# Decode block: the second part of w_up loaded in eleven smaller loads instead of one

## The chip, the cores and the metric

The kernel runs on one core of a Trainium2 chip. The metric is the device time of one execution in microseconds; before the change it is 204.33 us, the median of three runs (204.2, 204.33 and 204.76).

## The reference

One token goes through one block of a transformer in decode mode, all in bf16 at the boundary:

- x is one row of D = 640 numbers. It is normalised (layernorm without weights) and multiplied by wq (640 x 4096), which gives 32 queries of 128 numbers, one per head.
- Every head has its own cache of 4096 keys and 4096 values of 128 numbers. scores = q k / sqrt(128), softmax over the 4096 positions, and the weighted sum of the values.
- The 32 results together (4096 numbers) are multiplied by wo (4096 x 640) and added to x: this is h.
- h is normalised, g = h w_gate and u = h w_up (both 640 x 1728), gelu(g) * u is multiplied by w_down (1728 x 640) and added to h. This is the output, 640 numbers.

```python
h = x + _A_ref(_layernorm(x, axis=-1), A_k_cache, A_v_cache, A_wq, A_wo)
h2 = h + _B_ref(_layernorm(h, axis=-1), B_w_gate, B_w_up, B_w_down)
```

Each byte of the caches and of the weights is used once. They are about 84 MB.

## The kernel before

**How the program is written.** A small class `Sched` (L45) keeps five lists, one for each engine and one for SyncE (SP). `S.op` adds an instruction to an engine's list, `S.dma` adds a load, and both take the list of tokens that it must wait for. A token is a semaphore's name and a value. Each load slot has its own semaphore, named after the slot ("wu0", "wu1"). A wait that the engine has already made is left out. At the end the five lists are written out in the order in which they were filled. All loads but that of x are issued by SP, so the order of `S.dma` calls in the text is the order in which SP issues them.

**Attention.** The 32 heads are worked in NG = 8 groups of four. In a group each partition has 128 of the positions of one head. The keys of a group come in one load of 4 MB into `kbuf` (two buffers), the values in one load of 4 MB into `vbuf` (two buffers). For a group, `mult` (DVE, L324) multiplies the keys by the query, `fold` and `red` add the products up, `soft` makes the weights and `values` (PE, L380) applies them. `kfree[g]` is the token of the last `mult` of group g, `vfree[g]` that of its last `values`: a later load into the same buffer waits for it.

**The weights of the second half** have no room of their own. `wg_sb` (w_gate) lies over one key buffer, `wu_sb` (w_up) over the other, `wd_sb` (w_down) over a value buffer, `wo_sb` over that of wq. So their loads wait until the last groups have left these buffers. `wu_sb` is 128 partitions x 5 x 1728: partition p holds the rows 5p to 5p+4 of w_up.

**The loads at the end,** in the order of SP's list: three quarters of wo (L549); the values of the last group in two parts (L256); the last quarter of wo (L549); w_gate in one load (`pieces`, L543); w_up in two loads, rows 0 to 2 of each partition and rows 3 and 4 (`pieces` with the cuts [0, 3, 5], L543); and w_down: its last 64 rows (L561), then parts of 8, 4 and 1 blocks of 128 rows (L566). The loads of w_up wait for `kfree[7]`, those of w_down for `vfree[6]`. In the second load of w_up a partition takes 2 x 1728 numbers that lie in one piece in memory, 6912 bytes, and there are 128 such rows.

**Who uses them.** `up` (L617) multiplies the five pieces of h by w_gate, and then by w_up: for each of the five c in turn 14 matmuls, whose first waits for the token d_w[c]. So the 43rd of 70 matmuls with w_up is the first that needs the second load. PE's order after it: the rest of `up`, a small matmul with `twice` for the last 64 rows, and `down` (L659), which waits for each part of w_down. DVE's `hm` (L643) needs the whole of `up`. A last copy (L663) and a store of four rows (L664) end the kernel.

Of the kernel before, what the change touches and what calls it, by code (L numbers as in the profile page):

```python
# [16 lines left out]
NC_D = D // 128  # L17
# [6 lines left out]
NG = H // HG  # L24
# [85 lines left out]
def bass_sequential_preLN__gqa_block_cached__glu_gated_geglu__decode_kernel(  # L110
# [12 lines left out]
    S = Sched(nc)  # L123
# [10 lines left out]
    def over(name, base, shape):  # L134
        return nc.alloc_sbuf_tensor_at(name, shape, BF16, offset=nc.lookup_mloc(base).addr)
# [4 lines left out]
    wu_sb = over("wu_sb", kbuf[(NG + 1) % 2], [128, NC_D, DF])  # L140
# [88 lines left out]
    a = S.op("vector", lambda v: v.reduce_sum(  # L229
        jred[:, :], I32[:, :].rearrange("p (j c) -> p j c", c=HW), axis=AX.X))  # L230
    b = S.op("vector", lambda v: v.reduce_sum(
        cred[:, :], I32[:, :].rearrange("p (j c) -> p c j", c=HW), axis=AX.X))
# [11 lines left out]
    kfree, vfree = [None] * NG, [None] * NG  # L244
# [26 lines left out]
    def layernorm(src, t_src, o, dst, ps, beside=None):  # L271
        b = S.op("vector", lambda v: v.scalar_tensor_tensor(  # L272
            out=sq[:, :], in0=src[:, :], scalar=1.0, in1=src[:, :], op0=ALU.mult, op1=ALU.mult,
            accum_out=st[:, o + 1:o + 2]), [t_src])
        c = S.op("tensor", lambda t: t.matmul(ps[:, 0:2], part[:, :], st[:, o:o + 2],  # L275
                                              start=True, stop=True), [b, t_part])
        if beside is not None:
            beside()
        q = 2 * o
        d = S.op("vector", lambda v: v.scalar_tensor_tensor(  # L280
            out=ln[:, q:q + 1], in0=ps[:, 0:1], scalar=ps[:, 0:1], in1=eps[:, :],
            op0=ALU.mult, op1=ALU.subtract, reverse1=True), [c])
        e = S.op("scalar", lambda a: a.activation(  # L283
            ln[:, q + 1:q + 2], ps[:, 1:2], ACTF.Ln, bias=ln[:, q:q + 1]), [d])
        f = S.op("scalar", lambda a: a.activation(
            ln[:, q + 2:q + 3], ln[:, q + 1:q + 2], ACTF.Exp, scale=-0.5), [e])
        return S.op("vector", lambda v: v.tensor_scalar(  # L287
            dst[0], dst[1], ps[:, 0:1], ln[:, q + 2:q + 3], ALU.subtract, ALU.mult), [f])
# [250 lines left out]
    def pieces(slot, dst, src, cuts, waits):  # L539
        toks = []  # L540
        for i in range(len(cuts) - 1):
            lo, hi = cuts[i], cuts[i + 1]
            tok = S.dma("sync", "%s%d" % (slot, i), lambda s, lo=lo, hi=hi: s.dma_start(  # L543
                dst[:, lo:hi, :], src[:, lo:hi, :]), waits)
            toks += [tok] * (hi - lo)
        return toks

    def load_wo(lo, hi):
# [8 lines left out]
    d_wg = pieces("wg", wg_sb, B_w_gate[:, :].rearrange("(p c) n -> p c n", c=NC_D),  # L557
                  [0, 5], [kfree[NG - 2]])
    d_wu = pieces("wu", wu_sb, B_w_up[:, :].rearrange("(p c) n -> p c n", c=NC_D),
                  [0, 3, 5], [kfree[NG - 1]])  # L560
    d_wdr = S.dma("sync", "wdr", lambda s: s.dma_start(  # L561
        wd_sb[:, NFT, 0:D // 2], B_w_down[NFT * 128:DF, :].rearrange("r (h n) -> (r h) n", h=2)), [vfree[NG - 2]])
    d_wd = []
# [11 lines left out]
    def project(w):  # L575
        tok = None
        for c in range(HW):
            for cc in range(NC_D):
                last = w == NW - 1 and c == HW - 1 and cc == NC_D - 1
                first = w == 0 and c == 0 and cc == 0  # L580
                tok = S.op("tensor", lambda t, c=c, cc=cc, first=first, last=last: t.matmul(  # L581
                    pp[:, cc:cc + 1], wo_sb[:, w, c, cc::NC_D], aP[:, w * HW + c:w * HW + c + 1],
                    start=first, stop=last, skip_group_check=True),
                    [t_aP[w], d_wo[w], red_done[NG * NP - 2]], token=last)
        return tok
# [10 lines left out]
    b = project(w)  # L596
# [17 lines left out]
    t_hln = layernorm(h32, t_h, 2, (hln[:, :], h32[:, :]), pz, residual)  # L614


    def up(ps, w, d_w):  # L617
        b = None
        for c in range(NC_D):
            for s in range(NF):  # L620
                first = c == 0 and s == 0
                last = c == NC_D - 1 and s == NF - 1
                part = w[:, c, DF - 128:DF]
                if s < NFT:
                    b0, n, k = WD_COLS[s]
                    part = w[:, c, b0 + k:b0 + 128 * n:n]
                b = S.op("tensor", lambda t, s=s, c=c, part=part, first=first, last=last: t.matmul(
                    ps[:, s:s + 1], part, hln[:, c:c + 1],
                    start=first, stop=last, skip_group_check=True), [t_hln, d_w[c]], token=last)
        return b  # L630

    t_g = up(pg, wg_sb, d_wg)
    t_u = up(pu, wu_sb, d_wu)
    a = S.op("vector", lambda v: v.tensor_copy(g_t[:, :], pg[:, 0:NF]), [t_g])
    a = S.op("vector", lambda v: v.tensor_mul(t1[:, :], g_t[:, :], g_t[:, :]), [a])
    a = S.op("vector", lambda v: v.tensor_mul(t2[:, :], t1[:, :], g_t[:, :]), [a])
    a = S.op("vector", lambda v: v.scalar_tensor_tensor(
        out=t3[:, :], in0=t2[:, :], scalar=GELU_C1, in1=g_t[:, :], op0=ALU.mult, op1=ALU.add), [a])
    a = S.op("scalar", lambda a: a.activation(e_t[:, :], t3[:, :], ACTF.Exp, scale=-2.0 * GELU_C0), [a])
    a = S.op("vector", lambda v: v.tensor_scalar(d_t[:, :], e_t[:, :], 1.0, 0.0, ALU.add, ALU.add), [a])  # L640
    a = S.op("vector", lambda v: v.reciprocal(r_t[:, :], d_t[:, :]), [a])
    a = S.op("vector", lambda v: v.tensor_mul(gu[:, :], g_t[:, :], r_t[:, :]), [a])
    t_hm = S.op("vector", lambda v: v.tensor_mul(hm[:, :], gu[:, :], pu[:, 0:NF]), [a, t_u])  # L643

    b = S.op("tensor", lambda t: t.matmul(
        pz[:, 32:33], twice[:, :, :], hm[:, NFT:NF], start=True, stop=True), [t_hm, t_tw])
# [3 lines left out]
    def down(s, j):  # L650
        if s == NFT:
            return hr[:, j // 2:j // 2 + 1], wd_sb[:, NFT, j % 2 * NQ:(j % 2 + 1) * NQ]
        return hm[:, s:s + 1], wd_sb[:, s, j * NQ:(j + 1) * NQ]

    order = list(range(WD_PARTS[0])) + [NFT] + list(range(WD_PARTS[0], NFT))
    for i, s in enumerate(order):
        for j in range(4):
            last = i == NF - 1
            b = S.op("tensor", lambda t, s=s, j=j, last=last: t.matmul(  # L659
                pd[32 * j:32 * j + 1, 0:NQ], *down(s, j),  # L660
                start=False, stop=last, skip_group_check=True),
                [t_hr if s == NFT else t_hm, d_wd[s]], token=(last and j == 3))
# [35 lines left out]
```

## Time and profile before

| what | value |
|---|---|
| median of three runs | 204.33 us (204.2 to 204.76) |
| the profiled execution | 204.18 us, its span 202.9 us |
| TensorE's granted clock, mean | 0.919 |
| busy: PE, DVE, ACT | 77%, 57%, 15% of the span |
| read from memory | 84.23 MB, 415 GB/s over the span |
| second load of w_up | 864 KB, 26.4 us from issue to landing |
| loads of w_down | 23.4, 24.5 and 24.4 us from issue to landing; the last 64 rows 20.7 us |

All times below are of the profiled execution, in microseconds from the start of its span, if nothing else is said. A line of the chain or of the timeline begins with its start and its length. "SPq" is the queue of SP that issues loads; a line of it tells how long the issue took, not the transfer. In a line of the timeline the part in brackets is the engine's idle time before it and what ended it. The trace also keeps each DMA packet with its start, length and size (one packet is one row of a load, or a landing mark of 4 bytes), and the times at which a load's landing marks arrive: sixteen to a load of 128 rows, one from each DMA engine.

### The profile page before, as it was taken

Reading aid. Unit: us, or ns where it says so; the run is one execution under the profiler, and the core shown is the slowest. Engines: PE = TensorE matmul, PEld = TensorE weight load, DVE = VectorE, ACT = ScalarE, POOL = GpSimd, SP = SyncE. Lnnn points to the kernel's source line nnn. Section 1 sums busy time; section 2 is a strip of 40 time slices with the busy share of each in tenths; the row PEclk is TensorE's granted clock in tenths of the full one; section 3 lists DMA queues with packets and bytes.
Section 4 is the critical chain, followed back from the end, with each engine's and each line's share of the span. In section 5 each row is a group of like instructions: output and inputs, shape, how many; then the busy total and the mean of one; then the engine's idle time right before and its main releaser. Section 6 shows DMA issues by size and latency. Waiting matters only on the chain.

```text
span 202.9 us, 2478 instructions
## 1 busy us (share of the span) xinstructions
PE 155.8 (77%) x1069; PEld 73.2 (36%) x1075; DVE 115.9 (57%) x150; ACT 30.6 (15%) x110; POOL 1.2 (1%) x7
## 2 busy tenths in 40 slices
PE   0003649689959967999999499979768999996784
PEld 0001113233324322443343134424323344796682
DVE  5002087998099629883992588469999422301130
ACT  2000210006003300240060005100604013000000
POOL 1000000000000000000000000000000000000000
PEclk9999999999999996999999879999999999955555
DMA  6999999999999999999999999999999899999992
GB/s 250 420 460 413 413 439 465 439 413 413 436 446 452 420 409 420 436 434 459 413 413 426 452 449 420 420 420 420 471 433 423 381 430 458 404 422 417 415 420 87
DMA packets 4306, 84.38 MB, mean 416 GB/s; under 512 B 584, under 2 KB 840, under 8 KB 1096
## 3 DMA queue, kind: packets, MB, share of 16 engines
q1 hardware_dynamic: 4152, 84.23, 97.2%
q8 instruction: 8, 0.13, 0.3%
q10 hardware_dynamic: 144, 0.00, 0.0%
q14 instruction: 2, 0.02, 0.0%
HBM read 84.23 MB, written 0.00 MB: 415 GB/s over the span
## 4 chain that ended last, share of the span: by engine, by line
DMA 54%; DVE 28%; PE 14%; ACT 1%; issue 1%; SPq 0%
DMA kbuf<-in_A_k_cache_dram 34%; DVE prod L324 19%; DMA wd_sb<-in_B_w_down_dram 12%; DMA x_sb<-in_A_x_dram 8%; DVE sc L340 4%; PE pf L333 4%; PE pg L380 4%; PE pu L380 3%; PE pq L303 2%; DVE xz L397 2%; DVE xm L394 1%; ACT qb L309 1%; DVE mx L348 1%; DVE xb L287 0%; PE pf L659 0%
## 5 line engine op out<-in xcount | busy, mean ns | idle before, releaser
L324 DVE TENSOR_TENSOR prod<-kbuf,qb 128x4096 bf16<-128x4096 bf16 x32 | 72.8, 2278 | 32.8 <-DMA kbuf<-in_A_k_cache_dram 26.1
L333 PE MATMUL pf<-prod,Ibf 128*128 128x512 bf16 x256 | 65.7, 404 | 20.2 <-DVE prod L324 20.2
L333 PEld LDWEIGHTS pf<-prod,Ibf 128*128 128x128 bf16 x256 | 24.1, 102 | 58.9 <-DVE prod L324 26.8
L380 PE MATMUL pg<-vbuf,P 128*16 128x512 bf16 x128 | 29.9, 379 | 0.0
L340 DVE TENSOR_REDUCE sc<-pf 128x32 f32<-128x512 f32 x32 | 21.6, 676 | 5.1 <-PE pf L333 5.1
L380 PE MATMUL pu<-vbuf,P 128*16 128x512 bf16 x96 | 22.6, 384 | 0.0
L365 ACT ACTIVATE nb<-pm 128x4 f32<-128x4 f32 x8 | 1.4, 174 | 115.6 <-PE pm L362 115.6
L369 ACT ACTIVATE P<-sc,nb 32x128 bf16<-32x128 f32 x32 | 18.5, 578 | 0.9
L380 PEld LDWEIGHTS pg<-vbuf,P 128*16 128x16 bf16 x128 | 10.6, 89 | 14.5 <-issue 1.3
L275 PE MATMUL pz<-st,part 128*128 128x2 f32 x4 | 1.2, 363 | 17.2 <-DVE sq L272 17.2
L303 PE MATMUL pq<-wq_sb,xb 128*128 128x512 bf16 x34 | 10.8, 452 | 3.8 <-DVE xb L287 1.8
L380 PEld LDWEIGHTS pu<-vbuf,P 128*16 128x16 bf16 x96 | 8.3, 91 | 12.1 <-issue 2.3
L309 ACT CAST qb<-pq 32x128 bf16<-32x128 f32 x32 | 8.2, 257 | 6.5 <-PE pq L303 5.8
L369 ACT ACTIVATION_READ_ACCUMULATOR P<-sc,nb 32x1 f32 x32 | 8.0, 251 | 0.0
L581 PE MATMUL pf<-aP,wo_sb 128*128 128x1 bf16 x160 | 7.0, 178 | 0.7 <-issue 0.4
L290 DVE SCALAR_TENSOR_TENSOR x<-x_sb 128x5 f32<-128x5 bf16 x1 | 0.2, 166 | 12.7 <-DMA x_sb<-in_A_x_dram 12.7
L397 DVE TENSOR_REDUCE xz<-xm 16x128 f32<-16x512 f32 x7 | 7.3, 1040 | 0.2
L581 PEld LDWEIGHTS pf<-aP,wo_sb 128*128 128x128 bf16 x160 | 6.9, 132 | 1.2 <-issue 0.9
L275 PEld LDWEIGHTS pz<-st,part 128*128 128x128 f32 x4 | 1.0, 312 | 17.3 <-DVE sq L272 17.3
L303 PEld LDWEIGHTS pq<-wq_sb,xb 128*128 128x128 bf16 x40 | 3.8, 111 | 7.9 <-ACT qb L309 2.1
L283 ACT ACTIVATE ln<-pz,ln 128x1 f32<-128x1 f32 x2 | 0.5, 262 | 34.8 <-DVE ln L280 34.8
L394 DVE TENSOR_TENSOR xm<-pg,rmask 16x512 f32<-16x512 f32 x4 | 2.7, 671 | 3.4 <-PE pg L380 3.4
(78 smaller groups left out, 66.0 us busy)
## 6 DMA issues: line engine op xcount, KB each, us to landing
kbuf<-in_A_k_cache_dram SPq DMA_DIRECT2D x8, 4096.0 KB, 25.1
vbuf<-in_A_v_cache_dram SPq DMA_DIRECT2D x7, 4096.0 KB, 23.0
wq_sb<-in_A_wq_dram SPq DMA_DIRECT2D x1, 5120.0 KB, 15.3
wo_sb<-in_A_wo_dram SPq DMA_DIRECT2D x1, 3840.0 KB, 28.7
vbuf<-in_A_v_cache_dram SPq DMA_DIRECT2D x1, 3072.0 KB, 12.7
wg_sb<-in_B_w_gate_dram SPq DMA_DIRECT2D x1, 2160.0 KB, 22.2
wu_sb<-in_B_w_up_dram SPq DMA_DIRECT2D x1, 1296.0 KB, 24.8
wo_sb<-in_A_wo_dram SPq DMA_DIRECT2D x1, 1280.0 KB, 17.5
```

The source lines that it names most:

```text
L275: c = S.op("tensor", lambda t: t.matmul(ps[:, 0:2], part[:, :], st[:, o:o + 2], start=True, stop=True), [b, t_part])
L303: tok = S.op("tensor", lambda t, c=c, n0=n0: t.matmul(pq[:, :], xb[:, c, :], wq_sb[:, c, n0:n0 + HG * DH], start=(c == 0), stop=(c == NC_D ...
L309: t_qb[g] = S.op("scalar", lambda a, lo=lo, hi=hi, hh=hh: a.copy(qb[lo:hi, g, :], pq[lo:hi, hh * DH:(hh + 1) * DH]), [tok])
L324: return S.op("vector", lambda v: v.tensor_tensor(out=prod[n % NPR][:, :, :], in0=kbuf[g % 2][:, s * RP:(s + 1) * RP, :], in1=qb[:, g, :]. ...
L333: fold_done[n] = S.op("tensor", lambda t, j=j: t.matmul(pf[n % 2][:, :], Ibf[:, :], prod[n % NPR][:, :, j * W:(j + 1) * W], start=(j == 0) ...
L340: red_done[n] = S.op("vector", lambda v: v.reduce_sum(sc[g % 2][:, s * RP:(s + 1) * RP], pf[n % 2][:, :].rearrange("p (r w) -> p r w", r=R ...
L348: t_mx[g] = S.op("vector", lambda v: v.reduce_max(mx[:, g:g + 1], sc[g % 2][:, :], axis=AX.X), [red_done[g * NP + NP - 1]])
L369: t_exp[g] = S.op("scalar", lambda a, lo=lo, hi=hi, h=h, hh=hh: a.activation(P4[g % 2][lo:hi, :, hh], sc[g % 2][lo:hi, :], ACTF.Exp, bias= ...
L380: t_pv[g] = S.op("tensor", lambda t, i=i, r=r, last=last: t.matmul(pv[g % 2][0:VM, :], P4[g % 2][:, r:r + VR, :], vbuf[g % 2][:, r:r + VR, :],
L394: a = S.op("vector", lambda v: v.tensor_tensor(out=xm[:, :, :], in0=pv[g % 2][0:VM, :].rearrange("p (r d) -> p r d", r=VR), in1=rmask[:, : ...
L397: t_ext[g] = S.op("vector", lambda v: v.reduce_sum(xz[g % 2][:, :], xm[:, :, :].rearrange("p r d -> p d r"), axis=AX.X), [a, t_acc[g - 2] ...
L581: tok = S.op("tensor", lambda t, c=c, cc=cc, first=first, last=last: t.matmul(pp[:, cc:cc + 1], wo_sb[:, w, c, cc::NC_D], aP[:, w * HW + c ...
```

## The change

The second load of w_up is taken apart. Rows 3 and 4 of each partition (one piece of 6912 bytes) are now loaded so: for b = 0 to 6 one load takes the sixteen partitions b, 8 + b, 16 + b, ..., 120 + b. The sixteen partitions that are left, 7, 15, ..., 127, go in three loads of five and one load of one. These eleven loads have a semaphore each. `up` takes a list of tokens for the last two pieces of h and waits for all eleven before the 43rd matmul. The order of the other loads is as before, and what is computed is too.

```diff
     d_wu = pieces("wu", wu_sb, B_w_up[:, :].rearrange("(p c) n -> p c n", c=NC_D),
-                  [0, 3, 5], [kfree[NG - 1]])
+                  [0, 3], [kfree[NG - 1]])
+    rows = B_w_up[:, :].rearrange("(a b c) n -> b a c n", b=8, c=NC_D)
+    parts = [(b, 0, 16) for b in range(7)] + [(7, 0, 5), (7, 5, 10), (7, 10, 15), (7, 15, 16)]
+    d_wu += [[S.dma("sync", "wur%d_%d" % (b, lo), lambda s, b=b, lo=lo, hi=hi: s.dma_start(
+        wu_sb[8 * lo + b:8 * hi:8, 3:5, :], rows[b, lo:hi, 3:5, :]), [kfree[NG - 1]])
+        for b, lo, hi in parts]] * 2
     d_wdr = S.dma("sync", "wdr", lambda s: s.dma_start(
...
                 b = S.op("tensor", lambda t, s=s, c=c, part=part, first=first, last=last: t.matmul(
                     ps[:, s:s + 1], part, hln[:, c:c + 1],
-                    start=first, stop=last, skip_group_check=True), [t_hln, d_w[c]], token=last)
+                    start=first, stop=last, skip_group_check=True),
+                    [t_hln] + (d_w[c] if isinstance(d_w[c], list) else [d_w[c]]), token=last)
```

## The prediction

> **What bounds the kernel now.** I read the page's lines on the span and the DMA first, then the chain of work that ended last, then the queue of SP and the engines' timeline over the last 40 us, and then the packets and landing marks of single loads. The page:
>
> ```profile
> span 202.9 us, 2478 instructions
> ...
> PE 155.8 (77%) x1069; PEld 73.2 (36%) x1075; DVE 115.9 (57%) x150; ACT 30.6 (15%) x110; POOL 1.2 (1%) x7
> ...
> DMA  6999999999999999999999999999999899999992
> ...
> q1 hardware_dynamic: 4152, 84.23, 97.2%
> q8 instruction: 8, 0.13, 0.3%
> ```
>
> The reader should see that no compute engine is near full, while the sixteen DMA engines are busy from the second slice to the last but one: 97.2% of their time is SP's loads. 84.23 MB must come in, and the span is the time that takes, plus about 2 us at the front and 2.9 us behind the last landing. The chain's end:
>
> ```profile
> 174.66 0.33 SPq L561
> 174.99 0.04 issue
> 175.03 0.44 SPq L566
> 175.47 0.04 issue
> 175.51 24.47 DMA wd_sb<-in_B_w_down_dram
> 199.98 0.04 issue
> 200.02 0.87 PE pf L659 x20
> 200.89 0.02 issue
> 200.91 0.33 DVE o_sb L663
> ```
>
> The load on the chain took 24.47 us for 640 KB, because it stood in line: everything issued from 166.4 on is waiting in the same DMA engines. So what counts is when each DMA engine finishes its share, and the slowest one ends the kernel. The timeline, SP's issues and then the work around the changed load:
>
> ```profile
> 168.22 0.90 SPq L543 DMA_DIRECT2D wu_sb<-in_B_w_up_dram  x2
> 174.66 0.33 SPq L561 DMA_DIRECT2D wd_sb<-in_B_w_down_dram  x1
> 175.03 2.59 SPq L566 DMA_DIRECT2D wd_sb<-in_B_w_down_dram  x3
> 201.27 0.64 SPq L664 DMA_DIRECT2D out_dram<-o_sb  x1
> ...
> 193.48 3.53 PE L627 MATMUL pu<-hln,wu_sb 128*128 128x1 bf16 x70
> ...
> 197.12 0.17 DVE L643 TENSOR_TENSOR hm<-gu,pu 128x14 bf16<-128x14 f32 x1 [1.73 <-PE pu L627]
> ...
> 198.48 1.24 PE L659 MATMUL pf<-wd_sb,hm 128*1 128x160 bf16 x32 [0.95 <-DMA wd_sb<-in_B_w_down_dram]
> ```
>
> The changed load is the second of the two at 168.22 (its own issue at 168.69, 0.43 us). It lands at 195.1, and PE idles 0.95 us before 198.48 because W_down is late, not w_up.
>
> Two things come from the trace's records. Packets: all 128 rows of the changed load (6912 bytes each) took 0.262 to 0.267 us, and a landing mark 0.009 us. An instruction packet (16384 bytes) took 1.056 us on average, and each one sets one DMA engine back for good. Landing marks, sixteen to a load: those of the last load stand at 198.44, 198.60, 198.62, 198.66, 198.76, then eleven from 199.37 to 200.38. So five DMA engines end 1.6 to 1.9 us before the last one, and eleven are late.
>
> **The change part by part.**
>
> *Which engine carries what.* Before, each of 16 engines carries 8 rows. After, seven loads of sixteen rows give each engine 7. The last sixteen rows go five, five, five, one. The output (four rows) shows what a short load does: four packets, so one row each on four engines. A load of five rows then uses five engines. If these are the same five each time, they carry 10 rows, one of them 11, and the other eleven carry 7. In rows at full speed: eleven engines get 0.262 less, four get 2 x 0.262 = 0.52 more, one 3 x 0.262 = 0.79 more. The trace has no engine numbers, so it cannot say whether the five are the early five. [...] No run here shows the numbers.
>
> *Marks.* Each load leaves one mark on each engine it uses: seven instead of one is 6 x 0.009 = +0.05 us on every engine, +0.08 (nine or ten more) on the five.
>
> *The speed of a row.* Here the trace of before has no row that fits: under load every transfer covers 128 partitions, all engines side by side. The new loads write to sixteen partitions at a time, eight apart. Lower bound: the rows keep 0.262 us. Upper bound: two engines that meet in one place take turns, 0.52 us a row. The nearest rows of a packet that does not fit the even pattern: the instruction packets, 1.056 us for 16 KB or 66.0 ns per KB against 38.9 for a row, a factor of 1.70; and the first packets of wq, up to 2.43 us against 1.51, a factor of 1.60. The row of the very same size, 0.262, was measured under the old spread, which is just what is taken away, so I take 1.70, that is 0.445 us a row, and keep 1.0 and 2.0 for the range.
>
> At 1.70 the eleven need 7 x 0.445 + 0.05 - 8 x 0.262 = +1.07 us, four of the five 10 x 0.445 + 0.08 - 2.10 = +2.43, and one +2.88. If the five are the early ones, 1.62 us of theirs is free, so the end moves by 1.07 to 1.26 us. If the last engine is among them, by 2.43 to 2.88.
>
> [...]
>
> *SP.* Ten more issues: 11 x (0.43 + 0.04) = 5.2 us from 168.69, or 6.0 if the four short ones cost the output's 0.64. That ends at 173.9 to 174.7; SP then waits until 174.66 for PE's last values matmul anyway. W_down's loads are issued at most 0.1 us later. The last W_down issue took 1.64 us instead of 0.43, so the queue pushes back when much stands in it; with more loads in line it may be held some microseconds. Cover: that load moves its first row after 197, nearly 20 us later. Cost nothing; with the cover gone, W_down would be late one for one. The output's issue at 201.27 is far behind.
>
> *PE.* The 43rd matmul of up waits for eleven marks instead of one. The trace has no price; a load-and-multiply pair takes 3.5 / 70 = 0.05 us, so ten more waits lie between nothing and 10 x 0.05 = 0.5 us. Behind them stand 28 matmuls of up and all of down, and DVE's hm waits for those. Cover: the 43rd starts at 193.48 + 42 x 0.05 = 195.6, 0.5 after the landing, and 0.95 of idle time before 198.48. Cost nothing. If the rows land 1 to 2 us later, W_down behind them lands later by as much, so the cover stays.
>
> *Bytes* are the same; DVE, ACT and POOL are not touched.
>
> **Sum.** Everything behind is in line, so the slowest engine's delay goes straight to the end. I take the middle between the five being early (+1.1 to +1.3) and not (+2.4 to +2.9), about +1.8. The profiled execution took 204.18 us (202.9 and 1.3 around it), 0.15 under the median of 204.33: 204.33 + 1.8 = 206.1.
>
> **The rivals.**
>
> 1. *Rows at full speed and the five are the early ones.* Then the eleven late engines lose a row: -0.262 + 0.05 = -0.21, and the five end by 198.76 + 0.87 = 199.6, before the others. 204.1. For it: five early engines, and five rows. Against: the rows' new spread, and no engine numbers. This is the case on the other side, not slower; it decides as long as a row takes under (8 x 0.262 - 0.05) / 7 = 0.29 us.
>
> 2. *Rows at full speed, but the five include late engines.* The slowest moves by +0.4 to +0.9: 204.7 to 205.2. For it: eleven of sixteen are late, so five picked blindly would nearly surely include one within 0.4 us of the last. Against: the five that a short load takes may not be a blind pick.
>
> 3. *The slow rows are worse:* a factor of 2 on the loaded five, not early: 11 x 0.524 + 0.1 - 2.1 = +3.8, 208.1. For it: engines that collide also slow those that have not yet left an older load. Against: the engines are spread over 2 us, so pairs need not meet.
>
> 4. *More gain than a row:* an instruction packet falls on another engine or the end is set differently, -0.7 or better, 203.6. Nothing in the trace speaks for it but that the landing marks have 0.84 us between their mean (199.54) and the last.
>
> **How the numbers follow.** Slow rows by some 1.7: 0.50, 205.4 to 207.2. Rival 3: 0.10. Rival 2: 0.11, of which half lies beyond 0.3%. Rival 1: 0.22. Rival 4: 0.07. About 0.3% (0.6 us) is what a measurement of this kernel can tell from no change. Faster 0.07; same 0.22 + 0.06 = 0.28; slower 0.50 + 0.10 + 0.05 = 0.65. The range goes from the gain case, 204.0, to 207.4, between slow rows with the last engine hit (207.2) and rival 3; outside are rival 4 and most of rival 3. Within the likeliest case: 205.4 to 207.2.
>
> **What would show it.** Slow rows: packets of 6912 bytes with a median over 0.3 us, up to 0.52, and fewer GB/s than 418 between 191 and 196. Rival 1: packets at 0.262, and the last load's marks closer together, the early five gone. Rival 2: same packets, marks spread wider. The loads on SP ending before 174.7 shows that step right; a wait of PE or an idle DMA engine before W_down would show it wrong. The forecast falls if the row packets stay at 0.262 us.

## The result, and the profile after

The changed kernel takes 207.76 us (median of six runs, 207.18 to 208.5), the kernel before 204.21 us on the same chip (six runs, 204.01 to 204.76). The ratio is 1.0167, with a 95% interval from 1.0148 to 1.0186: 3.5 us slower. The profiled execution of the changed kernel is its fastest, 207.18 us, so the two traces are 3.0 us apart.

The page of the changed kernel:

```profile
span 205.9 us, 2499 instructions
...
PE 157.2 (76%) x1075; PEld 73.5 (36%) x1075; DVE 116.0 (56%) x150; ACT 30.6 (15%) x110; POOL 1.2 (1%) x7
...
DMA  7999999999999999999999999999999999999992
...
q1 hardware_dynamic: 4264, 84.23, 97.4%
```

The bytes are the same, the compute engines are the same, and the DMA engines are as busy as before, only for 3 us longer. The 112 packets more are the landing marks of ten more loads. The end of the chain:

```profile
176.39 0.42 SPq L571
176.81 0.04 issue
176.85 26.09 DMA wd_sb<-in_B_w_down_dram
202.95 0.04 issue
202.99 0.87 PE pf L665 x17
203.86 0.02 issue
203.88 0.32 DVE o_sb L669
```

It has the shape of before: W_down's second part lands, then 0.87 us of matmuls, then the copy. The landing has moved from 199.98 to 202.95. Where the time went shows when the span is cut into stages. First the kernel before; the last two columns are the busy share of the DMA engines and GB/s:

```profile
188.00:191.00 3.00, 1.90 (x28) 1.31 (x29) 0.52 (x2) 0.47 (x2) 0.05 (x1) 0.50 0.98 411
191.00:195.20 4.20, 4.20 (x89) 4.20 (x89) 1.11 (x6) 0.21 (x1) 0.00 (x0) 0.50 1.01 418
195.20:200.40 5.20, 3.74 (x92) 3.21 (x90) 0.50 (x3) 0.00 (x0) 0.00 (x0) 0.50 0.73 295
200.40:203.00 2.60, 0.46 (x16) 0.10 (x4) 0.33 (x1) 0.00 (x0) 0.00 (x0) 0.50 0.00 0
```

and the same stages of the changed kernel:

```profile
188.00:191.00 3.00, 2.15 (x29) 1.55 (x30) 0.52 (x2) 0.46 (x2) 0.32 (x1) 0.50 0.99 414
191.00:195.20 4.20, 3.02 (x62) 2.94 (x60) 1.11 (x6) 0.21 (x1) 0.00 (x0) 0.50 1.01 236
195.20:200.40 5.20, 3.32 (x67) 3.18 (x65) 0.17 (x1) 0.00 (x0) 0.00 (x0) 0.50 1.02 317
200.40:203.00 2.60, 1.56 (x40) 1.14 (x40) 0.33 (x2) 0.00 (x0) 0.00 (x0) 0.50 0.67 262
```

Until 191 the two are alike. Then, when the engines reach the changed rows, all sixteen stay fully busy and move 236 GB/s instead of 418. DMA engines that are busy the whole time (1.01) and move 0.56 of the bytes are the thing to see: nothing waits, the transfers themselves have become slow.

The packet records say which ones. Each figure is the extra time of all packets of one load against the kernel before, divided by sixteen, so per DMA engine:

| load | packet, before to after (mean) | extra per engine |
|---|---|---|
| first part of w_up (10368 bytes) | 0.394 to 0.452 us | +0.46 us |
| the changed rows (6912 bytes) | 0.262 to 0.457 us | +1.56 us |
| W_down's last 64 rows (640 bytes) | 0.032 to 0.057 us | +0.20 us |
| W_down's first part (10240 bytes) | 0.385 to 0.489 us | +0.83 us |
| landing marks (4 bytes) | 9 to 11 ns, and 112 more | +0.13 us |
| w_gate and the rest of W_down | | 0.0 us |
| sum | | +3.18 us |

The last landing mark moved from 200.38 to 203.34, by 2.96 us. So the sum of slower packets accounts for the change. Half of it is in the changed rows, and half in loads that were not touched and stand just before and behind them in line. Nothing earlier adds to it: the last mark of w_gate, the load before w_up, stands at 189.95 in both traces.

The times of the slow packets tie them to the changed rows, which move from 190.67 to 197.49. The 81 packets of w_up's first part that ended before 190.67 took at most 0.396 us, and the 26 that took over 0.42 all started after it, the first at 190.90. In W_down's first part 37 packets took over 0.42 us; the last of them ended at 198.22, and the 71 that started later took at most 0.393, although the engines were still some 2 us apart (its marks stand at 199.39 to 201.41). So in these two traces a load next in line is slow only while others are on the changed rows, or just after (198.22 against 197.49).

### The profile page after: what moved, and what is told of

Read it like the earlier page. It is cut to its first block, busy times and chain, and to the rows that moved or that the text cites. A ratio compares the mean times of both kernels' runs of the same rounds, so it can differ in the third digit from the quotient of the medians.

```text
span 205.9 us, 2499 instructions
## 1 busy us (share of the span) xinstructions
PE 157.2 (76%) x1075; PEld 73.5 (36%) x1075; DVE 116.0 (56%) x150; ACT 30.6 (15%) x110; POOL 1.2 (1%) x7
## 4 chain that ended last, share of the span: by engine, by line
DMA 54%; DVE 24%; PE 15%; SPq 4%; ACT 1%; issue 1%
DMA kbuf<-in_A_k_cache_dram 33%; DVE prod L324 16%; DMA wd_sb<-in_B_w_down_dram 13%; PE pf L333 8%; DMA x_sb<-in_A_x_dram 8%; PE pu L380 3%; DVE sc L340 3%; SPq L563 3%; PE pq L303 2%; DVE xz L397 2%; DVE xm L394 1%; ACT qb L309 1%; PE pg L380 1%; DVE xb L287 0%; PE pf L665 0%
## 5 line engine op out<-in xcount | busy, mean ns | idle before, releaser
L333 PE MATMUL pf<-prod,Ibf 128*128 128x512 bf16 x256 | 66.5, 408 | 20.1 <-DVE prod L324 20.0
L303 PE MATMUL pq<-wq_sb,xb 128*128 128x512 bf16 x40 | 12.1, 442 | 3.0 <-DVE xb L287 1.8
L632 PE MATMUL pu<-hln,wu_sb 128*128 128x1 bf16 x70 | 3.7, 187 | 3.0 <-DMA wu_sb<-in_B_w_up_dram 3.0
```

Source lines behind the costliest of these rows:

```text
L303: tok = S.op("tensor", lambda t, c=c, n0=n0: t.matmul(pq[:, :], xb[:, c, :], wq_sb[:, c, n0:n0 + HG * DH], start=(c == 0), stop=(c == NC_D ...
L333: fold_done[n] = S.op("tensor", lambda t, j=j: t.matmul(pf[n % 2][:, :], Ibf[:, :], prod[n % NPR][:, :, j * W:(j + 1) * W], start=(j == 0) ...
```

## The experiments

Three explanations were open. *Place*: a row is slow because of the partitions that a load takes at a time. *Many loads*: each further load costs something. *Five*: the last sixteen rows fall to five DMA engines, which finish late. Later a fourth, *count*: any load of fewer than 128 partitions is slow. Every kernel differs from the kernel before in the second part of w_up, if not said otherwise. The diffs are shortened: `rows` stands for the loads' partitions, first, end and step, and the line with a minus in the first one is the changed kernel's.

**Eight loads of sixteen partitions, dealt evenly** (e1_sixteens).

```diff
-    parts = [(b, 0, 16) for b in range(7)] + [(7, 0, 5), (7, 5, 10), (7, 10, 15), (7, 15, 16)]
+    rows = [(b, 128, 8) for b in range(8)]
```

> Eight loads of sixteen partitions eight apart; the last sixteen rows are one load like the others, so every DMA engine carries eight rows again. Theory 'place' (a row is slow because of the sixteen partitions that go at a time): rows still take 0.42 to 0.52 us, and the kernel stays 2 to 3.5 us above before, 206.3 to 207.8. Rival 'five' (the end is late because five engines carry ten or eleven rows): within 1 us of before, at most 205.2.

207.67 us, ratio 1.0168 (1.0131 to 1.0204); rows 0.495 us on average; the sum of slower packets, over the loads of the table, is 3.91 us per engine and the last landing moved by 3.94 (this profiled execution took 208.14). Without the loads of five the kernel is as slow as with them. *Five* is not the cause.

**Two halves** (e2_halves).

```diff
+    rows = [(0, 64, 1), (64, 128, 1)]
```

> The second part of w_up in two loads, partitions 0 to 63 and 64 to 127: only one load and one mark per engine more than before, and eight rows per engine as before. Theory 'place': rows of 0.42 to 0.52 us, 2 to 4 us above before, 206.2 to 208.2. Rival 'many loads' (each further load costs something of its own): 0.1 to 0.3 us above before, 204.3 to 204.5, rows of 0.262 us. [...]

207.46 us, ratio 1.0166 (1.0143 to 1.0188). One load more than before is enough for the whole loss. Rows take 0.439 us; the packets' sum is 2.72 us, the landing moved by 2.76. *Many loads* falls as the cause. The stages:

```profile
188.00:191.00 3.00, 1.76 (x20) 1.05 (x19) 0.61 (x6) 0.46 (x2) 0.47 (x1) 0.50 0.96 408
191.00:195.20 4.20, 3.89 (x78) 3.90 (x79) 0.49 (x3) 0.00 (x0) 0.00 (x0) 0.50 1.04 256
195.20:200.40 5.20, 3.42 (x66) 3.19 (x65) 1.37 (x8) 0.22 (x1) 0.00 (x0) 0.50 1.00 336
```

256 GB/s where the kernel before has 418: the pattern of the changed kernel with two loads.

**Eight loads over all partitions** (e3_columns).

```diff
+    wrows = B_w_up[:, :].rearrange("(p c) n -> p (c n)", c=NC_D)
+    wflat = wu_sb[:, :, :].rearrange("p c n -> p (c n)")
+    # eight loads
+        wflat[:, lo:lo + 432], wrows[:, lo:lo + 432]
```

> Eight loads as in e1_sixteens, but each of all 128 partitions and an eighth of the columns (864 bytes per row). Rival 'many loads': about as slow as e1_sixteens, 206 or more. Theory 'place': packets at 40 to 50 ns per KB instead of 38.9, so 0.1 to 0.6 us above before in all, 204.3 to 204.9.

204.79 us, ratio 1.0022 (1.0013 to 1.0032), 0.4 us. Packets of 864 bytes take 0.042 us, 49.8 ns per KB; 1024 of them come to 0.59 us more per engine than 128 rows of 6912 bytes. The loads beside them kept nearly their old speed: w_up's first part took 0.390 us (0.394 before), W_down's first part 0.393 (0.385 before). This run also answers a question on SP. Its queue:

```profile
168.37 0.43 SPq L543 DMA_DIRECT2D wu_sb<-in_B_w_up_dram  x1
168.84 18.85 SPq L563 DMA_DIRECT2D wu_sb<-in_B_w_up_dram  x8
187.73 2.31 SPq L566 DMA_DIRECT2D wd_sb<-in_B_w_down_dram  x1
190.09 2.33 SPq L571 DMA_DIRECT2D wd_sb<-in_B_w_down_dram  x3
201.77 0.62 SPq L670 DMA_DIRECT2D out_dram<-o_sb  x1
```

SP was held for almost 19 us with these eight issues, W_down was issued 13 us later than before, and the last landing moved by 0.5 us. So the 1.3 us by which the changed kernel issues W_down later cost nothing.

**The price of a row by itself** (e4_probe). The kernel before, and behind its output:

```diff
+    pats = [(0, 128, 1), (0, 128, 8), (4, 128, 8), (0, 112, 7), (0, 16, 1), (0, 64, 4), (7, 47, 8),
+            (127, 128, 1), (0, 64, 1), (0, 128, 4), (0, 128, 2), (0, 112, 1)]
+    # for each: four loads dst[lo:hi:step, c:c + 2, :], then SP waits for all four
```

> The kernel before, and behind its output twelve groups of four further loads of 6912-byte rows of w_up and w_gate over themselves, each group waited for before the next; all else is idle. It tells the price of a row by which partitions a load takes, with nothing else in the way. Theory 'place' by turns of two engines: all 128 partitions 0.262 us, sixteen that are eight apart 0.52, one row alone 0.262, 64 neighbouring partitions 0.45 to 0.52, five that are eight apart between. [...] If the price lies in the number of loads or in the other traffic, all groups show 0.262.

The stages of six of the groups, in this order: all 128 partitions; sixteen that are eight apart; sixteen neighbours; 64 neighbours; the 64 even ones; 112 neighbours. The compute engines are idle, so only the last two columns speak:

```profile
204.00:213.60 9.60, 0.00 (x0) 0.00 (x0) 0.00 (x0) 0.00 (x0) 0.00 (x0) 0.50 0.95 369
215.40:218.30 2.90, 0.00 (x0) 0.00 (x0) 0.00 (x0) 0.00 (x0) 0.00 (x0) 0.50 0.53 153
228.70:232.10 3.40, 0.00 (x0) 0.00 (x0) 0.00 (x0) 0.00 (x0) 0.00 (x0) 0.50 0.81 128
246.40:255.80 9.40, 0.00 (x0) 0.00 (x0) 0.00 (x0) 0.00 (x0) 0.00 (x0) 0.50 0.91 189
263.00:268.80 5.80, 0.00 (x0) 0.00 (x0) 0.00 (x0) 0.00 (x0) 0.00 (x0) 0.50 0.85 305
270.10:282.10 12.00, 0.00 (x0) 0.00 (x0) 0.00 (x0) 0.00 (x0) 0.00 (x0) 0.50 0.97 258
```

Where each engine has several rows, the records settle it: rows of all 128 partitions have a median of 0.262 us, of 64 neighbours 0.534 (2.04 times 0.262), of the 64 even partitions 0.262, of every fourth partition 0.262 (with a tenth of the rows at 0.58 or more), of 112 neighbours 0.395. Of the rows of sixteen neighbours the median is 0.583 and the slowest third takes about 1.0 us, almost four times 0.262.

The groups with one row per engine were a miss as a measurement. SP needs 0.63 us from one load of sixteen eight apart to the next, so the engines are idle half of the time there (busy 0.53 above). The medians are 0.38 to 0.43 us for sixteen eight apart, sixteen seven apart, sixteen four apart and five eight apart, and a single row that starts from rest takes up to 0.43 too. So these groups do not tell the patterns apart, and the expected 0.52 for sixteen eight apart was not seen.

**Even and odd partitions, and every fourth** (e6_evens, e5_fours).

```diff
+    rows = [(b, 128, 2) for b in range(2)]      # e6_evens
+    rows = [(b, 128, 4) for b in range(4)]      # e5_fours
```

> Two loads of 64 partitions as in e2_halves, but the even partitions and then the odd ones. If a load is slow because of which partitions go at a time (theory 'place'), these two, which reach over all 128, keep rows of 0.262 to 0.30 us as in the probe, and the kernel 204.3 to 205.0 us. If any load of fewer than 128 partitions is slow (rival 'count'), as slow as e2_halves: rows of 0.44 us, 207.0 to 207.8.

> Four loads of 32 partitions four apart. 'Place': in the probe half of these rows took 0.262 us and a tenth 0.58 and more, so rows between 0.262 and 0.35 and the kernel 204.5 to 206.0. 'Count': slower than e2_halves, rows over 0.44 us, 207.3 or more.

204.31 us, ratio 0.9994 (0.9983 to 1.0006), and 204.3 us, ratio 0.9997 (0.9981 to 1.0013). Rows take 0.262 and 0.266 us, and every load beside them has its old time; the fours are even a little better than was expected of them. The stages of e6_evens:

```profile
188.00:191.00 3.00, 1.67 (x26) 1.08 (x26) 0.52 (x2) 0.46 (x2) 0.00 (x0) 0.50 0.96 405
191.00:195.20 4.20, 4.20 (x90) 4.20 (x89) 1.03 (x6) 0.21 (x1) 0.00 (x0) 0.50 1.01 416
195.20:200.40 5.20, 3.69 (x89) 3.19 (x92) 0.58 (x4) 0.00 (x0) 0.00 (x0) 0.50 0.75 304
```

Beside e2_halves this is the clearest pair of the study. Two loads of 64 partitions, the same bytes and marks, eight rows per engine, and 256 against 416 GB/s; only which partitions go together differs. *Count* falls, *place* stands.

**Half the dose** (e7_half): the even partitions in one load, the odd ones in four loads that are eight apart.

```diff
+    rows = [(0, 128, 2)] + [(b, 128, 8) for b in (1, 3, 5, 7)]
```

> Half the dose: the even partitions in one load of 64, the odd ones in four loads of sixteen that are eight apart. If the cost goes with the number of slow rows alone, half of e1_sixteens: 1.4 to 1.8 us above before, 205.8 to 206.2. If it is set by the edges, where engines still on an older or already on a later load are met, more than two thirds: 2.3 us or more, 206.6 or more.

206.2 us, ratio 1.0105 (1.0057 to 1.0152): 1.9 us above before, against 3.3 for e1_sixteens. It lies nearer to half than to two thirds, but the interval of some 1 us on either side does not decide between them. The packets say more: 1.04 us per engine on the rows, with 92 of the 128 rows over 0.3 us, so at least 28 of the even rows were slowed too and the odd rows cannot be priced alone; 0.59 on W_down's first part and 0.13 on its last 64 rows; nothing on the first part of w_up, where only two packets took over 0.42 us instead of 26, now that the even rows, a fast pattern, stand between. The neighbours suffer where they touch slow rows.

**The dealing by itself** (e8_five): the kernel before, and the changed kernel's four short loads once more, into a buffer that nobody reads.

```diff
+    for lo, hi in ((7, 47), (47, 87), (87, 127), (127, 128)):
+        S.dma("sync", "five%d" % lo, ...
+            spare[lo:hi:8, 0:2 * DF], wrows[lo:hi:8, 3 * DF:5 * DF])
```

> The kernel before, and behind its second load of w_up the changed kernel's four short loads (five, five, five and one row of 6912 bytes) once more, into a buffer that nobody reads. Four of the five engines carry three rows more, one four. If the slowest engine is among them (rival 'five'): 3 to 4 x 0.262 = 0.8 to 1.1 us above before, 205.1 to 205.5, more if these rows are slow too. If the five end early enough: 204.3 to 204.6.

205.2 us, ratio 1.0051 (1.0034 to 1.0067): 0.95 us, within the 0.8 to 1.1 that late engines among the five would give. But that number took rows of 0.262 us, and 48 of the 144 rows took over 0.3. The slower and added packets sum to 1.1 us per engine over all sixteen (0.73 for rows, 0.35 for W_down's first part), so the time can be had without the five being late, and the run does not price the dealing. The landing marks show a mix: each short load's five marks fall into an early group (193.84 to 194.17 for the first) and a late one (194.91 and 195.15). That looks like three early and two late engines here, and two and three in the changed kernel.

**The dealing with the other rows fast** (e9_deal).

```diff
+    rows = [(0, 128, 4), (1, 128, 4), (2, 128, 4), (3, 128, 8), (7, 47, 8), (47, 87, 8), (87, 127, 8), (127, 128, 8)]
```

> The changed kernel's dealing of the last sixteen rows (five, five, five, one), but of the other 112 rows 96 in three loads of 32 partitions four apart, and sixteen in one load of partitions eight apart. The eleven engines carry six rows at 0.262 and one at 0.524, 2.10 us as before; the five carry two to three rows more. If the last sixteen are dealt to late engines: 0.6 to 1.5 us above before, 204.9 to 205.8. If they fall to early engines: 204.2 to 204.6. If the dealing costs what the whole change costs: 206.5 or more.

205.07 us, ratio 1.0041 (1.0026 to 1.0056), 0.8 us above before, as was expected for late engines among the five. Here too the packets offer another account: 64 of the 128 rows took over 0.3 us, and the extra time of rows (0.58 us per engine), W_down's first part (0.49) and the rest comes to 1.16, against a landing that moved by 0.93. What the run does show is the other side: with six of the seven rows per engine in a fast pattern, and the same dealing of the last sixteen, 2.7 of the 3.5 us of the change are gone.

## Why the prediction was wrong

The direction was right, and the rows became as slow as forecast (0.457 us against 0.445); one term of the sum was missing. 206.1 us with a range to 207.4 was forecast, an increase of 1.8 where 3.5 was measured.

- *The bound* was read rightly: the slowest DMA engine sets the end, and its delay went straight through. The last landing moved by 2.96 us, the profiled time by 3.0.
- *The speed of a row* was taken as 1.70 x 0.262 = 0.445 us from the instruction packets. Measured: 0.457, a factor of 1.74. No run ties the instruction packets to the changed rows, so the closeness is luck; e1_sixteens and e2_halves measured 0.495 and 0.439. The upper bound, 2 x 0.262 = 0.524, is what the halves of the probe show (0.534).
- *The term that was missing is the one that failed.* The sum priced the changed rows and their marks alone. That engines which collide also slow those still on an older load stood in the third rival without a price, and was answered there with "the engines are spread over 2 us, so pairs need not meet". The runs show the opposite. It cost 0.46 us per engine on the first part of w_up, 0.83 and 0.20 on W_down: 1.5 of the 3.18 us. The spread is what lets the loads meet. The changed rows moved from 190.67 to 197.49; the last packet of w_up's first part ended at 193.79, and the first of W_down's first part began at 193.89. So for 3.1 and for 3.6 us fast and slow patterns were on the way together.
- *The five.* The forecast split the outcome by whether the five are the early engines (+1.1 to +1.3) or include the last (+2.4 to +2.9). They were a mix, it seems, and that the loads of five take the same five engines each time was assumed: the traces have no engine numbers. The question mattered little: e1_sixteens deals evenly and is as slow. The middle of the two cases, +1.8, lies near the 1.56 us that the rows lost and the 0.13 of the marks, but it averaged two cases of which neither came: that is luck. Rival 2's 0.4 to 0.9 us for rows at full speed was not measured: in e8_five and e9_deal, which took 0.95 and 0.8 us more, a third and a half of the rows were slow.
- *Rival 3*, 208.1, lies nearer to the measured 207.76 than the forecast does, but its sum loads the end with eleven rows on one engine. e1_sixteens has eight rows on each and is as slow.
- *Rival 1*, a gain of 0.2, needed rows under 0.29 us; they took 0.457.
- *SP.* Eleven issues took 7.12 us, not 5.2 to 6.0: 0.57 to 0.80 for each load of sixteen or of five rows. W_down was issued 1.3 us later instead of 0.1, and the cover held, as e3_columns shows with 13.
- *PE.* The 43rd matmul started 0.56 us after the last of the eleven loads had landed (198.31, against 198.87), just above the 0 to 0.5 us given for ten more waits. A wait for one load, w_gate, ended 0.13 us after its last mark (189.95, 190.08), so the ten more cost some 0.43. The cover shrank and held: PE still idled 0.56 us for W_down before its first matmul (0.95 before):

```profile
198.87 1.51 PE L632 MATMUL pu<-hln,wu_sb 128*128 128x1 bf16 x28 [1.86 <-DMA wu_sb<-in_B_w_up_dram]
...
201.46 1.24 PE L665 MATMUL pf<-wd_sb,hm 128*1 128x160 bf16 x32 [0.56 <-DMA wd_sb<-in_B_w_down_dram]
```

That the set of partitions which go together sets the price is shown, by e6_evens beside e2_halves above all (0.262 against 0.439 us a row). Why it does is not shown: that two engines meet in one place and take turns was the author's estimate for the upper bound, and the traces do not tell which engine moves which row. Each pattern also changes which rows of w_up are read at the same time, and no run here separates where a row is read from where it is written.

## What to carry to other kernels

In a kernel bound by DMA, look at which partitions are in flight together and not at how many loads there are: here a full sweep, the evens and every fourth partition ran at 418, 416 and 413 GB/s from 191 to 195.2 (rows of 0.262, 0.262 and 0.266 us), while 64 neighbours and sixteen that are eight apart (e2_halves, e1_sixteens) ran at 256 and 226 (0.439 and 0.495 us). The slow pattern also slowed the loads before and behind it, by 0.46 and 1.03 us per engine in the changed kernel, while some engines were on it and others were not, so price the neighbours too. And full DMA engines with falling GB/s (1.01 busy, 236 instead of 418) meant slow transfers here, not a wait.

## What was not expected

- Splitting the load cost nothing by itself here, where the engines had work in line: two or four loads instead of one are within 0.1% (ratios 0.9994 and 0.9997). Eight loads with shorter rows cost 0.2%, and that SP was held in their issues for 18.85 us did no visible harm.
- A load of sixteen rows eight apart took SP 0.57 us or more to issue, w_up's first part with 128 rows 0.43, so such short loads did not keep idle DMA engines busy: 0.53 of their time in the probe.
- The slow patterns are also less steady: six runs of the changed kernel lie 1.3 us apart (207.18 to 208.5), six of the kernel before 0.75.
